# The router inside the attention loop: bias added in PSUM, one batch's operations over more steps, gathers three steps later

## The chip, the cores and the metric

One Trainium2 chip, one of its cores. The metric is the device time of one execution in microseconds (us); the median of several runs counts.

## The reference

Three stages follow each other: masked attention, a mixture of eight experts with a router (top 1), and a dense two-layer block. Cut to what matters here:

```python
# attention: q, k, v are (2, 8, 768, 64); a key counts where its 6-bit bucket equals the query's
mask = q_bucket[:, :, :, None] == k_bucket[:, :, None, :]
scores = np.where(mask, scale * np.matmul(q, k.transpose(0, 1, 3, 2)), -1000000000.0)
attn = np.exp(scores - scores.max(-1, keepdims=True))
attn = attn / (attn.sum(-1, keepdims=True) + 1e-09)
x = (attn @ v).transpose(0, 2, 1, 3).reshape(1536, 512)
# router and experts: x is (1536, 512), w_gate (512, 8), w1 (8, 512, 1024), w2 (8, 1024, 512)
logits = x @ w_gate + modality_bias[modality_id]
e_idx = np.argmax(logits, axis=1)
probs = np.exp(logits - logits.max(-1, keepdims=True))
probs /= probs.sum(-1, keepdims=True) + 1e-09
gate_w = probs[np.arange(N), e_idx]
for e in range(8):
    out[e_idx == e] = gate_w[e_idx == e, None] * (np.maximum(x[e_idx == e] @ w1[e], 0) @ w2[e])
# dense block: w_in (512, 2048), w_out (2048, 512)
h = out @ w_in
y = (np.maximum(h, 0.0) + alpha * np.minimum(h, 0.0)) @ w_out
```

## The kernel before

The attention runs as one loop of 102 steps, `s` from 0 to 101, that is written out by hand. A step takes one block of 128 keys of one head (6 blocks a head, 16 heads, so 96 blocks). For each block TensorE makes two halves of 384 scores (`ST`, tile `st`), ScalarE takes their exponential (`E`, L856) and rounds it to 16 bits (`Eh`, L860), and GpSimd makes the remainder E - Eh (`El`, L861, in `EL`). `EL(s-1)` is issued in step s. From block `ELD` = 88 on the remainder is made by VectorE instead of GpSimd; both of its inputs lie in SBUF. Every second step TensorE multiplies two blocks, Eh and El, with the values (`AV`, tile `av`, L869 to L871), four steps behind. `MAX` (tile `mxp`, L822) makes scores ahead for the row maxima, which VectorE reduces (L823). At the end of a head, `NORM` (L881 to L883) divides.

All small matmuls and transposes of the loop take their PSUM tile from `misc()`, a pool of PM = 2 buffers that also serves the router's scratch: whoever asks for a tile waits until the last user of the tile two requests ago is done. A score tile comes from a pool of five.

At the end of each step runs `hook(s)`. It builds the router (class `Router`) beside the attention. Batch 0 is complete halfway through the loop, so its routing (`first`) is done inside it: a generator that is advanced by one piece at each step listed in `PLAN["first"]`. Its pieces before: `S` (bias, maximum, exponential, argmax) at step 57; nothing at 58; the counting matmuls of `R` at 59; the ranks, counts and `star` (the fullest expert) at 60; `star2` at 63; `adjust` (14 operations on 128x6 elements) at 71; the one-hot matrix `HC` (`onehot`, L273) at 72; `GATE` at 75; `pre` in three pieces at 80, 81 and 83, the last of which writes the token numbers `idp`. GpSimd then gathers the first three tiles of tokens, one indirect DMA each (`GA`, L637), at steps 84, 85 and 87 (`PLAN["ga"]`). `TX0` transposes the gathered tiles at steps 96 and 97 (tile `g`, L602). Steps 91 to 100 also split the first expert's weights on ScalarE and VectorE (`W1`, L610 and L613). `T` and `L` in `hook` transpose x and make the logits `lg` (L182, L185, L196, L200).

Batch 1 is routed after the loop by the same `S`, `R`, `adjust` and `GATE` (tiles `tr`), between the first matmuls of the experts.

Each engine works through its instructions in the order in which they are issued. So a waiting instruction holds everything behind it on its engine. In `S` before, the bias is added by one VectorE operation with both inputs in SBUF, and the result goes to PSUM:

```python
v.tensor_tensor(out=w, in0=self.lg[:, bs], in1=self.tb[:, bs], op=ALU.add)   # L213
```

Of the kernel before, what the change touches and what calls it, by code (L numbers as in the profile page):

```python
# [12 lines left out]
I32 = mybir.dt.int32  # L13
AF = mybir.ActivationFunctionType
ALU = mybir.AluOpType
# [23 lines left out]
PM = 2  # L39
PLAN = dict(  # L40
    v0=(1, 3, 4), T3=(2, 2), Z3=(5, 6), T=(2, 4, 5, 7), Z=(8, 10), ld1=9, ld=0, am1=(12, 12, 13, 13), am=(4, 6, 8,
    10), sc=(13, 15), tot=3, tot0=6, sp=(-2, 4, 10, 18), cap=(3, 2, 0, 1), x=(1, 2, 7, 3), x3=(0, 1, 2, 2), x4=(9, 10, 13, 11), w1=(91, 92, 95, 96, 97, 98, 99, 100), ga=(84, 85, 87), vl=1, am0=(0, 0), Z2=(0, 1), x6=(0, 1, 6, 4), first=(57, 58, 59, 60, 63, 71, 72, 75, 80, 81, 83),
)
NPRE = 3
NT = 22
NBASE = 13
GROUPS = ((0, 1, 2), (3, 4, 5), (6, 7, 8, 9), (10, 11, 12))
NG = NT - NPRE
ELD = 88
LOW = 2.0 ** -15  # L50
HIGH = float(np.uint32(0x47EFFFFF).view(np.float32))

# [5 lines left out]
class Router:  # L58
# [145 lines left out]
    def S(self, b, ps):  # L204
        nc = self.nc
        v = nc.vector
        bs = slice(6 * b, 6 * b + 6)
        s8 = [128, 6, 8]
        p = ps()
        w = p[:, 0:48].rearrange("p (c e) -> p c e", c=6)  # L210
        eq = p[:, 64:112].rearrange("p (c e) -> p c e", c=6)
        pe = p[:, 112:118]
        v.tensor_tensor(out=w, in0=self.lg[:, bs], in1=self.tb[:, bs], op=ALU.add)  # L213
        mx = self.tmp([128, 6, 1], F32, "lmx")
        v.tensor_reduce(out=mx, in_=w, axis=AX.X, op=ALU.max)
        v.tensor_tensor(out=eq, in0=w, in1=mx.to_broadcast(s8), op=ALU.is_equal)
        v.tensor_tensor(out=w, in0=w, in1=mx.to_broadcast(s8), op=ALU.subtract)
        ex = self.tmp(s8, F32, "ex")
        nc.scalar.activation(ex, w, AF.Exp)
        v.scalar_tensor_tensor(out=eq, in0=eq, scalar=-16.0, in1=self.iota16.unsqueeze(1).to_broadcast(s8), op0=ALU.mult, op1=ALU.add)  # L220
        v.tensor_reduce(out=pe, in_=eq, axis=AX.X, op=ALU.min)
        v.tensor_tensor(out=self.oh[:, bs], in0=self.iota[:, 0:8].unsqueeze(1).to_broadcast(s8), in1=pe.unsqueeze(2).to_broadcast(s8), op=ALU.is_equal)
        v.tensor_copy(self.e[:, bs], pe)
        self.ex = ex
        yield
# [101 lines left out]
    def adjust(self, b, ps):  # L327

        v = self.nc.vector
        bs = slice(6 * b, 6 * b + 6)  # L330
        p = ps()
        e, r, pf, rp, f = (p[:, 8 * i:8 * i + 6] for i in range(5))
        si, qi = (p[:, 8 * i:8 * i + 6].bitcast(I32) for i in (5, 6))
        v.tensor_copy(e, self.e[:, bs])
        v.tensor_copy(r, self.r[:, bs])
        isS = self.isS[:, bs]
        v.tensor_scalar(out=isS, in0=e, scalar1=self.es, scalar2=None, op0=ALU.is_equal)
        if b == 0:
            v.scalar_tensor_tensor(out=pf, in0=r, scalar=128.0 * NPRE, in1=isS, op0=ALU.is_lt, op1=ALU.mult)
            v.tensor_scalar(out=self.np_[:, bs], in0=pf, scalar1=-1.0, scalar2=1.0, op0=ALU.mult, op1=ALU.add)  # L340
            v.tensor_tensor(out=isS, in0=pf, in1=isS, op=ALU.not_equal)
        v.tensor_copy(f, isS)
        rps = self.rp[:, bs]
        v.scalar_tensor_tensor(out=rps, in0=f, scalar=self.nm0, in1=self.r[:, bs], op0=ALU.mult, op1=ALU.add)
        v.tensor_copy(si, rps)
        v.tensor_scalar(out=qi, in0=si, scalar1=7, scalar2=None, op0=ALU.logical_shift_right)
        v.tensor_scalar(out=si, in0=si, scalar1=127, scalar2=None, op0=ALU.bitwise_and)
        v.tensor_copy(self.rq[:, bs], qi)
        v.tensor_copy(f, si)
        v.tensor_copy(self.rm[:, bs], si)  # L350
        yield
        self.onehot(self.HC[:, bs], f, 6)

    def pre(self, ps):

        nc = self.nc
        v = nc.vector
        p = ps()
        rq, q, rc = p[:, 256:262], p[:, 264:270], p[:, 288:288 + 6 * NPRE].rearrange("p (c t) -> p c t", c=6)
        v.tensor_copy(rq, self.rq[:, 0:6])  # L360
        s = [128, 6, NPRE]
        v.scalar_tensor_tensor(out=q, in0=self.np_[:, 0:6], scalar=100.0, in1=rq, op0=ALU.mult, op1=ALU.add)
        v.tensor_tensor(out=rc, in0=self.iota[:, 0:NPRE].unsqueeze(1).to_broadcast(s), in1=q.unsqueeze(2).to_broadcast(s), op=ALU.is_equal)
        rv = self.tmp([128, 6, 4, NPRE], F16, "prv")
        s4 = [128, 6, 4, NPRE]
        v.tensor_tensor(out=rv, in0=rc.unsqueeze(2).to_broadcast(s4), in1=self.vals[:, 0:6].unsqueeze(3).to_broadcast(s4), op=ALU.mult)
        yield
        for c in range(6):
            nc.tensor.matmul(p[:, 0:4 * NPRE], self.HC[:, c], rv[:, c].rearrange("p a t -> p (a t)"), start=(c == 0), stop=(c == 5))
        yield  # L370
        self.gates_of(p, NPRE, self.idp, self.gp)
# [125 lines left out]
def _program(base, tc, nc, q, k, v, proj, mod, w_gate, mbias, w1, w2, win, wout, alpha, out):  # L497
# [359 lines left out]
    def EL(s):  # L857
        j=s%6; e,eh,el=E[s]
        if s in (91,94): nc.vector.tensor_copy(eh,e)
        else: nc.scalar.activation(eh,e,AF.Copy)  # L860
        (nc.vector if s>=ELD else nc.gpsimd).tensor_tensor(out=el,in0=e,in1=eh,op=ALU.subtract)  # L861
    av={};xs={}
# [698 lines left out]
```

## Time and profile before

| what | value |
|---|---|
| runs | 692.78, 699.09, 698.83 us; median 698.83 us |
| the profiled execution | 698.25 us, of which the span of its instructions is 696.5 us |
| TensorE busy | 662.4 us, 95% of the span |
| VectorE, ScalarE, GpSimd busy | 450.4 us (65%), 315.8 us (45%), 237.6 us (34%) |
| mean granted clock of TensorE | 0.979 of full speed |

The busy shares are over the whole span. The attention loop takes about the first 262 us; behind it come the experts and then the dense block. A granted clock of 1.00 in a row is 2.4 GHz, 0.50 is 1.2 GHz.

### The profile page before, as it was taken

The numbers are of one execution on the slowest core, as the hardware profiler recorded it, in microseconds if no ns is written. First come the engines' busy times: TensorE is split into PE (matmuls) and PEld (weight loads), VectorE is DVE, ScalarE is ACT, GpSimd is POOL, SyncE is SP. The second block draws the span as 40 slices with busy tenths as digits, with TensorE's granted clock in tenths as the row PEclk, the third lists the DMA queues.
The fourth block names the chain that finished last, engine by engine and source line by source line (L and its number), as shares of the span: only waits on it lengthen the run. The fifth ranks groups of instructions, "written<-read, shape, count | busy, mean of one in ns | idle before, by whom it ended". The sixth has DMA issues, their size and how long they took to land.

```text
span 696.5 us, 12779 instructions
## 1 busy us (share of the span) xinstructions
PE 662.4 (95%) x4938; PEld 562.7 (81%) x4938; DVE 450.4 (65%) x925; ACT 315.8 (45%) x536; POOL 237.6 (34%) x212
## 2 busy tenths in 40 slices
PE   7797999998999899999999999999999999999996
PEld 6586998997878789789888887888888888888884
DVE  6877788788888587846642757999543444443332
ACT  5565797885867863223512337675411111111111
POOL 8775999986966800401000201040030000100002
PEclk9979999999999989999999999999999999999999
DMA  8367855866511309757311643533010000000001
GB/s 215 87 148 173 183 134 115 177 175 145 115 37 49 121 3 333 252 202 276 106 60 61 213 157 130 177 89 128 0 68 24 6 26 0 31 30 1 1 0 60
DMA packets 32859, 75.02 MB, mean 108 GB/s; under 512 B 7276, under 2 KB 7366, under 8 KB 32534
## 3 DMA queue, kind: packets, MB, share of 16 engines
q1 hardware_dynamic: 29700, 64.43, 32.3%
q0 software_dynamic: 2960, 9.70, 4.2%
q8 instruction: 39, 0.64, 0.4%
q14 instruction: 30, 0.25, 0.1%
q10 hardware_dynamic: 130, 0.00, 0.0%
HBM read 49.79 MB, written 14.68 MB: 93 GB/s over the span
## 4 chain that ended last, share of the span: by engine, by line
PE 53%; DVE 1%; ACT 1%; issue 1%; POOL 1%; ACTq 0%; POOLq 0%
PE o L1406 18%; PE h L1380 18%; PE y L1067 8%; PE g L1047 8%; PE tr L1250 1%; POOL out_dram L1423 1%; PE tr L1034 0%; DVE w L1225 0%; DVE op L1225 0%; ACT op L1223 0%; DVE gl L613 0%; ACT gf L1384 0%; ACT q L1385 0%; ACT w L1223 0%; DVE big L1190 0%
## 5 line engine op out<-in xcount | busy, mean ns | idle before, releaser
L861 POOL TENSOR_TENSOR El<-E,Eh 128x768 f16<-128x768 f32 x88 | 144.4, 1651 | 44.1 <-ACT Eh L860 23.2
L856 ACT ACTIVATE E<-st 128x384 f32<-128x384 f32 x192 | 89.2, 492 | 63.1 <-PE st L855 60.8
L823 DVE TENSOR_REDUCE mx<-mxp 128x1 f32<-128x384 f32 x192 | 97.8, 548 | 10.0 <-PE mxp L822 9.2
L610 ACT ACTIVATE gh<-gf 128x512 fp32r<-128x512 f32 x48 | 30.3, 631 | 142.8 <-PE o L1406 132.2
L860 ACT ACTIVATE Eh<-E 128x768 f16<-128x768 f32 x94 | 79.6, 846 | 0.0
L854 PE MATMUL st<-op 97*128 97x384 f32 x192 | 74.8, 390 | 0.6 <-ACT E L856 0.6
L822 PE MATMUL mxp<-op 76*128 76x384 f32 x192 | 66.7, 361 | 7.5 <-DMA op<-big 2.7
L613 DVE TENSOR_TENSOR gl<-gf,gh 128x512 fp32r<-128x512 f32 x48 | 33.1, 690 | 59.2 <-ACT gh L610 59.2
L1423 POOL DMA_INDIRECT out_dram<-x,did x12 | 11.8, 986 | 167.8 <-DVE x L1420 89.1
L1380 PE MATMUL h<-big,op 128*128 128x512 f32 x256 | 67.9, 393 | 0.0
L855 PE MATMUL st<-op 128*128 128x384 f32 x192 | 67.4, 351 | 0.0
L1406 PE MATMUL o<-op,gh 128*128 128x512 f32 x192 | 64.2, 395 | 0.0
L871 PE MATMUL av<-vh,El 128*128 128x65 f16 x576 | 60.0, 197 | 1.9 <-POOL El L861 1.9
L869 PE MATMUL av<-vh,Eh 128*128 128x65 f16 x576 | 60.8, 199 | 0.2 <-DVE big L883 0.2
L870 PE MATMUL av<-vl,Eh 128*128 128x64 f16 x576 | 60.2, 196 | 0.0
L869 PEld LDWEIGHTS <-Eh 128*128 128x128 f16 x576 | 53.7, 100 | 7.7 <-issue 6.4
L1238 POOL DMA_INDIRECT yg<-ys,dpos x10 | 12.2, 1215 | 138.4 <-DVE x L1190 73.0
L1067 PE MATMUL y<-op,hh 128*128 128x512 f32 x172 | 58.7, 399 | 0.0
L1380 PEld LDWEIGHTS h<-big,op 128*128 128x128 f32 x256 | 48.1, 188 | 10.9
L871 PEld LDWEIGHTS <-El 128*128 128x128 f16 x576 | 54.3, 100 | 2.2 <-POOL El L861 2.2
L870 PEld LDWEIGHTS <-Eh 128*128 128x128 f16 x576 | 54.4, 101 | 0.0
L1388 DVE TENSOR_SCALAR gf<-h,al 128x512 f32<-128x512 f32 x33 | 24.8, 751 | 41.7 <-PE h L1380 41.7
(423 smaller groups left out, 1490.7 us busy)
## 6 DMA issues: line engine op xcount, KB each, us to landing
r<-in_moe_w_dram SPq DMA_DIRECT2D x14, 1024.0 KB
op<-B SPq DMA_DIRECT2D x32, 192.0 KB
op<-A SPq DMA_DIRECT2D x28, 192.0 KB
op<-A SPq DMA_DIRECT2D x13, 384.0 KB
ys<-zero SPq DMA_DIRECT2D x19, 256.0 KB
op<-in_moe_w_in_dram SPq DMA_DIRECT2D x4, 1024.0 KB
op<-in_moe_w_out_dram SPq DMA_DIRECT2D x4, 1024.0 KB
ys<-ysb SPq DMA_DIRECT2D x13, 256.0 KB
```

What stands on the lines that cost most here:

```text
L823: nc.vector.tensor_reduce(out=mx[h][:,c,a:a+1],in_=p[:,0:384],axis=AX.X,op=ALU.max)
L854: mm(p[:,0:384],t[0:97,1,js],t[0:97,2,qs],start=True,stop=False)
L855: mm(p[:,0:384],t[:,0,js],t[:,3,qs],start=False,stop=True)
L856: nc.scalar.activation(E[s][0][:,qs],p[:,0:384],AF.Exp,scale=0.125)
L860: else: nc.scalar.activation(eh,e,AF.Copy)
L861: (nc.vector if s>=ELD else nc.gpsimd).tensor_tensor(out=el,in0=e,in1=eh,op=ALU.subtract)
L869: mm(a[:,c*65:c*65+65],eh[:,cs],VH[h//4%2][:,j,h%4,:],start=(j==0 and c==0),stop=False,skip_group_check=True)
L870: mm(a[:,c*65:c*65+64],eh[:,cs],VL[h//4%2][:,j,h%4,:],start=False,stop=False,skip_group_check=True)
L871: mm(a[:,c*65:c*65+65],el[:,cs],VH[h//4%2][:,j,h%4,:],start=False,stop=False,skip_group_check=True)
L1067: nc.tensor.matmul(yps[key][i], a[:, ts], w[:, c], start=(c == 0 and m == 0), stop=(c == 7 and m == 2))
L1380: nc.tensor.matmul(p, terms[t][0][:, kk, cs], terms[t][1][:, kk], start=(n == 0), stop=(n == 11))
L1406: nc.tensor.matmul(po[b][i], a[:, ts], w[:, c % 2], start=(c == 0 and n == 0), stop=(c == 15 and n == 2))
```

## The change

- `S`: `lg` is first copied to the PSUM tile `w`, then `tb` is added there. Holds for both batches.
- `adjust`: in batch 0 a new pause splits it in two, with a new PSUM tile behind it; the one-hot matrix gets a PSUM tile of its own, to which `rm` is copied back. In batch 1 the copy of `r` is no longer made. `pre` takes a new tile for its matmuls.
- `PLAN["first"]`: S at 57, nothing at 58, R at 59 and 60 as before; `star2` at 66 (63 before); `adjust` at 72 and 75 (71); one-hot at 78 (72); `GATE` at 83 (75); `pre` at 84, 85 and 86 (80, 81, 83).
- `PLAN["ga"]`: the gathers at steps 87, 88 and 90 (84, 85, 87).
- `ELD` = 87: the remainder of block 87 too is made by VectorE.

```diff
-    ... ga=(84, 85, 87), ... first=(57, 58, 59, 60, 63, 71, 72, 75, 80, 81, 83),
+    ... ga=(87, 88, 90), ... first=(57, 58, 59, 60, 66, 72, 75, 78, 83, 84, 85, 86),
...
-ELD = 88
+ELD = 87
...
-        v.tensor_tensor(out=w, in0=self.lg[:, bs], in1=self.tb[:, bs], op=ALU.add)
+        v.tensor_copy(w, self.lg[:, bs])
+        v.tensor_tensor(out=w, in0=w, in1=self.tb[:, bs], op=ALU.add)
...
-        e, r, pf, rp, f = (p[:, 8 * i:8 * i + 6] for i in range(5))
-        si, qi = (p[:, 8 * i:8 * i + 6].bitcast(I32) for i in (5, 6))
+        e, r, pf = (p[:, 8 * i:8 * i + 6] for i in range(3))
         v.tensor_copy(e, self.e[:, bs])
-        v.tensor_copy(r, self.r[:, bs])
...
         if b == 0:
+            v.tensor_copy(r, self.r[:, bs])
...
             v.tensor_tensor(out=isS, in0=pf, in1=isS, op=ALU.not_equal)
+            yield
+            p = ps()
+        f = p[:, 24:30]
+        si, qi = (p[:, 8 * i:8 * i + 6].bitcast(I32) for i in (5, 6))
         v.tensor_copy(f, isS)
...
-        v.tensor_copy(f, si)
         v.tensor_copy(self.rm[:, bs], si)
         yield
+        p = ps()
+        f = p[:, 0:6]
+        v.tensor_copy(f, self.rm[:, bs])
         self.onehot(self.HC[:, bs], f, 6)
...
         yield
+        p = ps()
         for c in range(6):
             nc.tensor.matmul(p[:, 0:4 * NPRE], self.HC[:, c], rv[:, c].rearrange("p a t -> p (a t)"), start=(c == 0), stop=(c == 5))
```

## Rows read from the trace of the kernel before

**Rows 1.** The page, part 2: the granted clock in 40 slices of 17.4 us.

```profile
PEclk9979999999999989999999999999999999999999
```

**Rows 2.** Waits of TensorE, 150 to 265 us: waiting line, releaser, us, times, longest.

```profile
PE misc L795 <- DVE r L881: 2.6, 1, 2.6
PE av L871 <- POOL El L861: 1.9, 1, 1.9
...
PE misc L182 <- DVE big L273: 0.8, 1, 0.8
...
PE misc L182 <- DVE big L185: 0.3, 1, 0.3
```

**Rows 3.** Timeline of VectorE around L213: start us, duration us, instruction.

```profile
162.32 2.52 DVE L213 TENSOR_TENSOR misc<-lg,tb 128x48 f32<-128x48 f32 x1
164.88 0.21 DVE L215 TENSOR_REDUCE lmx<-misc 128x6 f32<-128x48 f32 x1
...
166.48 0.16 DVE L223 COPY e<-misc 128x6 f32<-128x6 f32 x1
...
266.56 0.22 DVE L213 TENSOR_TENSOR tr<-lg,tb 128x48 f32<-128x48 f32 x1
```

**Rows 4.** Timeline of GpSimd, three stretches; in brackets the idle time before.

```profile
158.28 6.49 POOL L861 TENSOR_TENSOR El<-E,Eh 128x768 f16<-128x768 f32 x4
...
196.48 3.36 POOL L861 TENSOR_TENSOR El<-E,Eh 128x768 f16<-128x768 f32 x2 [1.74 <-PE mxp L822]
...
235.26 0.98 POOL L637 DMA_INDIRECT big<-x_d,idp  x1 [0.17 <-issue]
236.26 3.26 POOL L861 TENSOR_TENSOR El<-E,Eh 128x768 f16<-128x768 f32 x2
239.68 1.51 POOL L637 DMA_INDIRECT big<-x_d,idp  x1 [0.16 <-issue]
241.20 1.65 POOL L861 TENSOR_TENSOR El<-E,Eh 128x768 f16<-128x768 f32 x1
```

**Rows 5.** Timeline of VectorE, 196 to 206 us.

```profile
198.71 0.15 DVE L334 COPY misc<-e 128x6 f32<-128x6 f32 x1
...
199.36 0.17 DVE L339 SCALAR_TENSOR_TENSOR misc<-misc,isS 128x6 f32<-128x6 f32 x1
...
202.40 0.94 DVE L273 TENSOR_TENSOR big<-iota,misc 128x768 f16<-128x768 f32 x1
```

**Rows 6.** Stretches: length, busy us of each engine, granted clock, DMA share, GB/s.

```profile
164.20:166.80 2.60, 0.01 (x1) 0.04 (x2) 2.13 (x9) 1.18 (x4) 0.56 (x1) 1.00 1.00 214
168.20:171.60 3.40, 3.40 (x45) 3.10 (x45) 3.31 (x7) 1.71 (x3) 2.27 (x2) 0.50 0.00 0
...
200.00:206.00 6.00, 4.50 (x65) 3.56 (x64) 5.63 (x19) 3.40 (x7) 3.25 (x2) 1.00 0.11 18
...
243.30:250.10 6.80, 6.80 (x67) 6.31 (x64) 5.95 (x10) 3.48 (x7) 0.00 (x0) 0.50 0.02 5
```

**Rows 7.** Timeline of VectorE: where it waited after 170 us and after 238 us.

```profile
172.64 1.09 DVE L823 TENSOR_REDUCE mx<-mxp 128x1 f32<-128x384 f32 x2 [1.09 <-PE mxp L822]
...
238.74 1.60 DVE L861 TENSOR_TENSOR El<-E,Eh 128x768 f16<-128x768 f32 x1 [1.56 <-ACT Eh L860]
...
241.65 2.03 DVE L861 TENSOR_TENSOR El<-E,Eh 128x768 f16<-128x768 f32 x1 [0.84 <-ACT Eh L860]
...
249.04 0.96 DVE L861 TENSOR_TENSOR El<-E,Eh 128x768 f16<-128x768 f32 x1 [0.68 <-ACT Eh L860]
...
252.78 0.96 DVE L861 TENSOR_TENSOR El<-E,Eh 128x768 f16<-128x768 f32 x1 [0.62 <-ACT Eh L860]
```

**Rows 8.** Timeline of ScalarE: the rounding of block 87.

```profile
236.25 0.85 ACT L860 ACTIVATE Eh<-E 128x768 f16<-128x768 f32 x1
```

**Rows 9.** Timeline of TensorE: the first transposes of gathered tokens.

```profile
253.71 1.07 PE L602 MATMUL g<-ident,big 128*128 128x128 f32 x8
```

**Rows 10.** Instructions on tile idp: time from the gathers' issue to landing.

```profile
DMA to landing us min/median/max: 3.3/3.6/4.0
```

More of the change, by code (lines that the diff above doesn't have):

```diff
@@ L41 @@
     v0=(1, 3, 4), T3=(2, 2), Z3=(5, 6), T=(2, 4, 5, 7), Z=(8, 10), ld1=9, ld=0, am1=(12, 12, 13, 13), am=(4, 6, 8,
-    10), sc=(13, 15), tot=3, tot0=6, sp=(-2, 4, 10, 18), cap=(3, 2, 0, 1), x=(1, 2, 7, 3), x3=(0, 1, 2, 2), x4=(9, 10, 13, 11), w1=(91, 92, 95, 96, 97, 98, 99, 100), ga=(84, 85, 87), vl=1, am0=(0, 0), Z2=(0, 1), x6=(0, 1, 6, 4), first=(57, 58, 59, 60, 63, 71, 72, 75, 80, 81, 83),
+    10), sc=(13, 15), tot=3, tot0=6, sp=(-2, 4, 10, 18), cap=(3, 2, 0, 1), x=(1, 2, 7, 3), x3=(0, 1, 2, 2), x4=(9, 10, 13, 11), w1=(91, 92, 95, 96, 97, 98, 99, 100), ga=(87, 88, 90), vl=1, am0=(0, 0), Z2=(0, 1), x6=(0, 1, 6, 4), first=(57, 58, 59, 60, 66, 72, 75, 78, 83, 84, 85, 86),
 )
```

## The prediction

> **What bounds the kernel now.** I read the busy shares first: TensorE is busy nearly throughout, so a change on the other engines can move the time only where TensorE waits for them, or where its clock falls. The row of the granted clock [rows 1] is next: in the attention (the first 15 slices) it dips in few places, the last of them in the slice from 244 us. Then come TensorE's waits over the stretch in which the router runs beside the attention [rows 2]. Two stand out, and both end at engines that the change touches: 2.6 us for VectorE at a `misc` tile, and 1.9 us for GpSimd's remainder El. The others are below 1.2 us; two of them, 0.8 and 0.3 us, are again for `misc` tiles that VectorE has not given back.
>
> The first wait is explained by one instruction. L213, the addition of the bias, took 2.52 us in the loop and 0.22 us after it [rows 3], for the same shape. In the loop GpSimd was making four remainders without a pause, from 158.28 to 164.77 us [rows 4], and L213 ended at 164.84, right behind them. So an operation of VectorE with both inputs in SBUF waits here until GpSimd's stream ends. A later case agrees: VectorE's remainder that starts at 241.65 took 2.03 us instead of the 0.96 of its fellows [rows 7], and GpSimd's last remainder ended at 242.85 [rows 4], 0.83 us before it. Operations with one input in PSUM do not wait: the copy L334 (0.15 us) and L339 (0.17 us) ran at 198.71 and 199.36 [rows 5], inside a GpSimd pair of remainders that lasted from 196.48 to 199.84 [rows 4].
>
> What L213 holds up is S, whose last reader L223 ends at 166.64 [rows 3]; TensorE's Z matmul needs S's `misc` tile and stands from 164.18 to 166.79 [rows 2, 6]. Soon after, the granted clock is 0.50 (1.2 GHz) from 168.2 to 171.6 us, with TensorE busy all of it [rows 6]. The second wait has the same sequel: GpSimd does gather, remainders 85 and 86, gather, remainder 87 in its order [rows 4]; remainder 87 ends at 242.85, TensorE stands for 1.9 us [rows 2], and from 243.3 to 250.1 us the clock is 0.50, TensorE again busy throughout [rows 6]. Each sequel is work at half rate: 3.4 us that could be 1.7, and 6.8 us that could be 3.4.
>
> **The change part by part.** The sum is made against the profiled execution, 698.25 us; that is 0.6 us below the median of the three runs.
>
> *Bias in PSUM.* L213 becomes a copy (SBUF to PSUM) and an addition with one PSUM input. Both are forms that rows 5 show unhindered beside GpSimd. From L213 to L215 went by 2.56 us [rows 3]; two instructions at 0.25 each, the spacing of such small ones (0.22 us run [rows 3], plus a few hundredths), make 0.5. S then ends 2.05 us earlier, and TensorE's 2.61 us wait shrinks to 0.55. Term A: -2.05 us. Bounds: nothing if the copy waits for GpSimd as the addition did, 2.61 if S were done in time altogether.
>
> *Half clock after it.* With 0.55 us of wait I expect no fall: the 1.5 us that TensorE is idle from 200 to 206 us left the clock at 1.00 [rows 6]. On TensorE alone that gives 1.7 us. But VectorE is busy 3.31 of those 3.4 us [rows 6], and its next idle time is the 1.09 us before 172.64 [rows 7], behind which it is loaded again; it can come forward by A and this idle time, no more. Term B: -1.09 us, bounds 0 and -1.70.
>
> *Operations spread.* adjust is 14 operations in one go, from 198.71, the first of rows 5, until 201.5; after two row maxima the one-hot of 0.94 us follows [rows 5], and TensorE waits 0.8 us for the tile that this chain holds and then 0.3 for the next [rows 2]. After the change six operations come at step 72, seven at 75, and the one-hot at 78 with a tile of its own; no tile is held over several steps. The work itself is the same 14 operations and the one-hot, some 3.9 us at these durations; star2, GATE and pre also only move to later steps, GATE and pre behind the last row maxima, where VectorE has room: before remainder 88 alone it stood 1.56 us [rows 7]. Term C: -1.0 us, the two waits. Bounds: 0 (each new tile brings a wait of its own, since there are still two) and -1.5, all that TensorE is idle in that stretch [rows 6].
>
> *Gathers later and remainder 87 on VectorE.* GpSimd's last remainder is now 86, and no gather stands ahead of any. Eh of block 87 is there at 237.10 [rows 8]. VectorE is free then (idle until 238.74 [rows 7]); GpSimd, without its gathers of about 1 to 1.5 us each [rows 4], has finished remainders 85 and 86 by about 237.3. So El 87 takes 0.96 us [rows 7] and is there by about 238.3, hidden in the 1.56 us of idle time; if a GpSimd remainder is still running, add up to 1.65 [rows 4], which the next idle time of 0.84 covers only in part. TensorE asked for it at 241.0. The wait of 1.88 us goes, and with it, I expect, the half clock: 1.88 + 3.40 = 5.28 us on TensorE. It can't have all of that, since VectorE is next: from 241.65 to the loop's end it is nearly always busy. What it can shed is the wait inside the remainder that starts at 241.65 (2.03 - 0.96 = 1.07) and its three idle times behind it, 0.68, 0.64 and 0.62, of which rows 7 show the first and the last: 3.0 us together. Term D: -3.0 us, bounds -1.07 and -5.28.
>
> What is queued behind the moved instructions: behind the gathers on GpSimd nothing of the loop any more; behind El 87 on VectorE remainder 88 and a transposed copy. The gathers land 3.6 us after issue [rows 10]; issued three steps later, at about 238 to 242, the last lands by about 246, and TX0 begins at 253.71 [rows 9], or some 7 us earlier once everything has moved. That still holds. In batch 1, behind the loop, S gets one copy and adjust loses one, at about 0.2 each: nothing.
>
> Sum: 698.25 - 2.05 - 1.09 - 1.0 - 3.0 = 691.1 us. After the loop nothing is tied to absolute time, since its loads are issued there; so I let the whole sum arrive at the end.
>
> A rule that speaks against the later gathers: the Trainium skill, page "SBUF — State Buffer", section "SBUF: two separate sides", says that GpSimd can't write the descriptors of its DMAs while VectorE runs an operation that takes their shared ports. The gathers now meet VectorE's remainders, so by this rule they come later. The trace has one such meeting: the gather at 239.68, beside a remainder of VectorE until 240.34, took 1.51 us against 0.98 for the one at 235.26 [rows 4, 7], 0.5 us more. Three such meetings are 1.6 us, which the distance to TX0 covers. What a stronger form would do is the last rival.
>
> **The rivals.** *Only the waits, not the clock, and the gain is taken back by VectorE and ScalarE.* The steps between 172 and 241 us are close to balanced, and an earlier TensorE may just wait more often there. Then A and the smaller end of D remain, 2.05 + 1.07, and some 0.5 of B and C: about 694.6 us. For it: VectorE's 5.63 busy of 6 us from 200 to 206 [rows 6]. Against it: VectorE waited for TensorE at 172.64 [rows 7] and GpSimd for it at 196.48 [rows 4], so they have slack too.
>
> *More than the sum.* If VectorE's order lets TensorE have all of B and C and most of D, the upper bounds give 2.05 + 1.70 + 1.5 + about 4.5 = 9.75, or 688.5 us. The run at 692.78 among the three of before speaks for it: something of the order of 6 us comes and goes with nothing changed, about the 5.1 us of both half-clock stretches, and the waits would then still be there to be removed.
>
> *The change doesn't do what it says.* The copy reads SBUF in single precision; if it waits for GpSimd like L213, A and B vanish and a copy is added: 698.25 - 1.0 - 3.0 + 0.2 = 694.5 us. The copy L334 [rows 5] speaks against it.
>
> *Slower: the gathers starve.* From 244.66 until about 261 us VectorE runs two-input operations on SBUF nearly back to back (remainders, weight splits). If a gather can't get in between them at all, the three come after 261 us and land at about 261 + 3 x 1.0 + 3.6 = 268 instead of before 253.71 [rows 4, 9, 10]; TX0, and behind it everything on TensorE, waits 14 us. With the 7.2 gained elsewhere that is 705 us. It begins to cost when the last gather lands later than TX0, some 2 to 8 us later than I reckon, and ends slower than before from about twice 7 us. Against it stand the 1.51 us of the gather that met a remainder [rows 4].
>
> **How the numbers follow.** About 1% of 698.8 us, 7 us, is what a measurement can tell from no change. Chances: the forecast (689.5 to 693) 0.50, the gain taken back 0.24, more than the sum 0.16, the copy that waits 0.05, the starving gathers 0.05. Predicted time 691.1 us. Range 687.5 to 695.5: from the upper bounds to the taken-back gain and the copy that waits. The forecast lies just at 1% faster than the median, so its half and the larger gain make faster 0.48, the rest and the two cases near 694.5 make the same 0.47, slower 0.05.
>
> **What the profile afterwards would show.** L213's copy and addition at about 0.2 us each with GpSimd busy beside them; no wait of 2 us at L795; granted clock 1.00 in the slices behind 160 and behind 240 us; remainder 87 on VectorE at about 1 us, no TensorE wait for GpSimd's El; gathers unbroken behind GpSimd's last remainder; the loop's end (the last NORM) at about 255 instead of 261 us. The prediction is wrong if the copy takes over 1 us, if a new TensorE wait of 2 us or more stands between 200 and 240 us and brings the clock down again, or if L602 waits for a gather.

## The result and the profile after

The changed kernel takes 689.29 us (median; 687.33 to 690.03), the kernel before 698.46 us in the same comparison: ratio 0.9887, 95% interval 0.9853 to 0.9922, so 0.8 to 1.5% faster. A second comparison gave 689.46 us and 0.9892 (0.9850 to 0.9935). The profiled execution took 690.03 us, its span is 688.2 us; the prediction was 691.1 us.

The waits of TensorE in the same stretch of the changed kernel (lines are 1 to 7 higher, since the file has grown):

```profile
PE mxp L829 <- ACT E L863: 1.4, 3, 0.5
PE av L876 <- DVE big L890: 1.3, 1, 1.3
PE g L590 <- DVE op L613: 0.8, 1, 0.8
PE tr L182 <- DVE big L890: 0.7, 1, 0.7
...
PE misc L802 <- DVE r L888: 0.6, 1, 0.6
```

The two waits on which the prediction rested [rows 2] are 0.6 us (it was 2.6) and gone. The longest single one left is new: the product `av` of head 15 waits for VectorE's division of head 14. The waits for the one-hot's tile (0.8 and 0.3) are gone as well. The first line, three short waits for ScalarE, was there before too, with 1.5 us in all.

VectorE at the bias, the answer to [rows 3]:

```profile
162.40 0.19 DVE L213 COPY misc<-lg 128x48 f32<-128x48 f32 x1
162.69 0.22 DVE L214 TENSOR_TENSOR misc<-misc,tb 128x48 f32<-128x48 f32 x1
162.94 0.21 DVE L216 TENSOR_REDUCE lmx<-misc 128x6 f32<-128x48 f32 x1
...
164.55 0.16 DVE L224 COPY e<-misc 128x6 f32<-128x6 f32 x1
```

GpSimd, the answer to [rows 4]:

```profile
158.35 6.49 POOL L868 TENSOR_TENSOR El<-E,Eh 128x768 f16<-128x768 f32 x4
...
229.44 3.26 POOL L868 TENSOR_TENSOR El<-E,Eh 128x768 f16<-128x768 f32 x2 [1.37 <-ACT Eh L867]
232.88 1.69 POOL L644 DMA_INDIRECT big<-x_d,idp  x1 [0.18 <-issue]
234.87 0.97 POOL L644 DMA_INDIRECT big<-x_d,idp  x1 [0.30 <-issue]
236.14 0.95 POOL L644 DMA_INDIRECT big<-x_d,idp  x1 [0.30 <-issue]
```

GpSimd's four remainders run as before, at the same time and with the same 6.49 us; the copy and the addition run beside them at 0.19 and 0.22 us, where one addition took 2.52. The gathers stand behind the last remainder, in one go.

And the granted clock over the whole execution, the answer to [rows 1]:

```profile
PEclk9979999999999999999999999999999999999998
```

The dip in the slice from 244 us is gone in this execution.

Where the time came from is read best from three events on VectorE: the start of the bias in S, the division of head 13 and that of head 15, the last of the loop. Before, L213 starts at 162.32 [rows 3], and the divisions at

```profile
234.88 0.23 DVE L881 TENSOR_SCALAR r<-av,sc 128x6 f32<-128x6 f32 x1 [1.64 <-PE av L875]
...
260.88 0.22 DVE L881 TENSOR_SCALAR r<-av,sc 128x6 f32<-128x6 f32 x1
```

(timeline of VectorE, kernel before), after the change at

```profile
230.20 0.23 DVE L888 TENSOR_SCALAR r<-av,sc 128x6 f32<-128x6 f32 x1 [0.89 <-PE av L882]
...
252.65 0.22 DVE L888 TENSOR_SCALAR r<-av,sc 128x6 f32<-128x6 f32 x1
```

So S to head 13 took 72.56 us and takes 67.80 (4.76 less), head 13 to head 15 took 26.00 and takes 22.45 (3.55 less). What follows until the end of the span is 435.6 and 435.55 us: nothing is lost or won behind the loop. The sum of the two, 8.3 us, is the difference of the spans.

### The profile page after: what moved, and what is told of

It reads as the page before. It is cut to its first block, busy times and chain, and to the rows that moved or that the text cites. A ratio compares the mean times of both kernels' runs of the same rounds, so it can differ in the third digit from the quotient of the medians.

```text
span 688.2 us, 12777 instructions
## 1 busy us (share of the span) xinstructions
PE 658.1 (96%) x4938; PEld 558.1 (81%) x4938; DVE 446.9 (65%) x927; ACT 315.2 (46%) x536; POOL 235.8 (34%) x211
## 4 chain that ended last, share of the span: by engine, by line
PE 54%; DVE 1%; ACT 1%; issue 1%; POOL 1%; ACTq 0%; POOLq 0%
PE o L1413 19%; PE h L1387 18%; PE y L1074 8%; PE g L1054 8%; PE tr L1257 1%; POOL out_dram L1430 1%; PE tr L1041 0%; DVE w L1232 0%; DVE op L1232 0%; ACT op L1230 0%; DVE gl L620 0%; ACT gf L1391 0%; ACT q L1392 0%; ACT w L1230 0%; DVE big L1197 0%
## 5 line engine op out<-in xcount | busy, mean ns | idle before, releaser
L868 POOL TENSOR_TENSOR El<-E,Eh 128x768 f16<-128x768 f32 x87 | 142.8, 1655 | 38.9 <-ACT Eh L867 20.5
L620 DVE TENSOR_TENSOR gl<-gf,gh 128x512 fp32r<-128x512 f32 x48 | 33.1, 690 | 59.2 <-ACT gh L617 57.2
L876 PE MATMUL av<-vh,Eh 128*128 128x65 f16 x576 | 58.9, 197 | 1.3 <-DVE big L890 1.3
L876 PEld LDWEIGHTS <-Eh 128*128 128x128 f16 x576 | 52.8, 99 | 8.5 <-issue 6.1
L877 PE MATMUL av<-vl,Eh 128*128 128x64 f16 x576 | 58.4, 194 | 0.0
L878 PE MATMUL av<-vh,El 128*128 128x65 f16 x576 | 58.2, 195 | 0.0
L877 PEld LDWEIGHTS <-Eh 128*128 128x128 f16 x576 | 53.4, 99 | 0.0
```

The source lines that it names most:

```text
L876: mm(a[:,c*65:c*65+65],eh[:,cs],VH[h//4%2][:,j,h%4,:],start=(j==0 and c==0),stop=False,skip_group_check=True)
L877: mm(a[:,c*65:c*65+64],eh[:,cs],VL[h//4%2][:,j,h%4,:],start=False,stop=False,skip_group_check=True)
L878: mm(a[:,c*65:c*65+65],el[:,cs],VH[h//4%2][:,j,h%4,:],start=False,stop=False,skip_group_check=True)
```

## The experiments

Single executions of one kernel differ: the 72 of the kernel before that ran beside the experiments lie between 692.96 and 702.09 us. Each has a mean granted clock with it, and the two go together (correlation -0.93): 693.04 at 0.990, 702.09 at 0.974. One straight line with a common slope through 169 executions of all kernels (one of 2297 us, at a clock of 0.283, is left out) gives 0.35 us of time for each us that the clock was at half rate; what it leaves over scatters by 0.95 us. So each kernel has two figures below: its median, and its difference from the kernel before at an equal mean clock, with the 95% half-width of the fit; between two of the other kernels the half-width is 0.8 to 1.1 us. The stage lengths are from one profile each, with the time at half clock in them, which comes as 0, 3.4 or 6.8 us.

| kernel | median us | at equal clock, us | S to head 13 (half clock) | head 13 to 15 (half clock) |
|---|---|---|---|---|
| before | 696.78 (72 executions) | 0 | 72.56 (3.4) | 26.00 (6.8) |
| changed | 689.30 (10) | -6.3 ± 0.6 | 67.80 (0), again 67.75 (0) | 22.45 (0), again 22.83 (3.4) |
| x1 bias in PSUM alone | 694.42 (10) | -1.7 ± 0.6 | 69.66 (0) | 26.00 (6.8) |
| x2 late gathers alone | 695.48 (10) | -1.2 ± 0.6 | 71.31 (0) | 22.72 (0) |
| x3 remainder 87 on VectorE alone | 697.36 (10) | -1.2 ± 0.6 | 71.30 (0) | 24.73 (6.8) |
| x4 spread and late gathers | 693.42 (10) | -3.3 ± 0.6 | 71.55 (6.8) | 22.72 (0) |
| x5 changed, bias from SBUF | 690.89 (4) | -3.5 ± 1.0 | 71.67 (6.8) | 24.03 (6.8) |
| x6 changed, remainder 87 on GpSimd | 690.35 (8) | -5.6 ± 0.7 | 67.81 (0) | 22.69 (0) |
| x7 before, own tile for S | 697.46 (10) | -0.4 ± 0.6 | 73.20 (6.8) | 23.81 (0) |

**x1: the bias in PSUM alone.**

```diff
-        v.tensor_tensor(out=w, in0=self.lg[:, bs], in1=self.tb[:, bs], op=ALU.add)
+        v.tensor_copy(w, self.lg[:, bs])
+        v.tensor_tensor(out=w, in0=w, in1=self.tb[:, bs], op=ALU.add)
```

> Only the bias: the kernel before with the copy into PSUM and the addition there. My theory (the addition with two SBUF inputs waits for GpSimd's stream, and the wait costs TensorE time and then half clock): the copy and the addition take about 0.2 us each, the 2.6 us wait at L795 falls to about 0.6, the clock stays at 1.00 behind it, and what follows comes 2.7 us earlier, also at the loop's end: about 695.7 us beside 698.5. The 1.9 us wait for GpSimd's El of block 87 and the half clock behind it stay. Rival (the steps from 172 to 241 us are balanced and take the gain back): within 0.7 us of before at the loop's end.

Measured: ratio 0.9963 (0.9936 to 0.9989). Waits of TensorE:

```profile
PE av L872 <- POOL El L862: 1.9, 1, 1.9
...
PE misc L796 <- DVE r L882: 0.6, 1, 0.6
```

The wait fell as expected, the one for GpSimd's El stayed, and the stage up to head 13 is 2.9 us shorter than in the kernel before, and 1.65 us shorter than in x2 and x3, which have the old addition and no half clock. So the wait itself is worth 1.65 us, and the 3.4 us of half clock in the profile of before another 1.25.

**x2 and x3: the two edits at block 87, one at a time.**

```diff
-... ga=(84, 85, 87)
+... ga=(87, 88, 90)      # x2
-ELD = 88
+ELD = 87                 # x3
```

> Only the gathers at steps 87, 88, 90; remainder 87 stays on GpSimd. My theory (the gathers in front of GpSimd's last remainders make El 87 late): only one gather now stands ahead of El 87, which ends at about 240.3 instead of 242.85, before TensorE asks for it at 241.0; wait and half clock go, the loop ends about 3 us earlier, 695.5 us. Rival (it is the move of El 87 to VectorE that matters): the 1.9 us wait stays or moves, no change, 698.5 us.

> Only remainder 87 on VectorE, gathers at their old steps. My theory: VectorE starts El 87 at about 237.2 but must wait for GpSimd's pair 85 and 86, which the second gather holds back to 239.5, so El 87 is there at about 240.5, just before TensorE asks at 241.0; the wait goes or is under 0.5 us, the half clock goes too, about 2.5 us gained, 696 us. Rival (both parts are needed): VectorE falls behind by the 3.3 us of that operation, TensorE waits for a VectorE remainder instead, with half clock behind it: 698 to 700 us.

Measured: 0.9994 (0.9961 to 1.0027) and 1.0003 (0.9970 to 1.0037), no difference in the ratios; 1.2 us each at equal clock. GpSimd in x2:

```profile
234.77 3.27 POOL L861 TENSOR_TENSOR El<-E,Eh 128x768 f16<-128x768 f32 x2 [0.44 <-ACT Eh L860]
238.22 1.18 POOL L637 DMA_INDIRECT big<-x_d,idp  x1 [0.18 <-ACT E L856]
239.44 1.67 POOL L861 TENSOR_TENSOR El<-E,Eh 128x768 f16<-128x768 f32 x1
```

El 87 is the single remainder. It ends 5.6 us after the division of head 13 (235.55 in x2), against 8.0 in the kernel before, and TensorE no longer waits for it. In x3 VectorE did wait for GpSimd's pair, and longer than a single remainder lasts; VectorE first, then GpSimd:

```profile
233.81 3.15 DVE L861 TENSOR_TENSOR El<-E,Eh 128x768 f16<-128x768 f32 x1 [1.27 <-ACT Eh L860]
236.89 0.54 DVE L185 COPY big<-misc 128x384 f32<-128x384 f32 x1
```

```profile
232.88 3.26 POOL L861 TENSOR_TENSOR El<-E,Eh 128x768 f16<-128x768 f32 x2
```

VectorE's El 87 began in the first of the pair and came out 0.8 us after the second (236.14). In x3 a new wait of 1.3 us for VectorE (at L196) took the old one's place, with 6.8 us of half clock behind it. In x2 TensorE waits for VectorE too, at L869 (the division of head 14) and at L196, with no half clock behind it in this profile:

```profile
PE av L869 <- DVE big L883: 1.5, 2, 1.3
...
PE misc L196 <- DVE lg L200: 0.7, 1, 0.7
```

The kernel before waits at L869 for at most 0.2 us and at L196 not at all; x7, which has the wait for El 87 without half clock, waits 1.0 us at L869. Both edits are worth the same where the other is missing, since each by itself removes the wait for El 87, and shorter ones for VectorE come instead. The size that both expectations gave, 2.5 to 3 us, was too large: it contained the half clock, and it did not reckon with these waits.

**x4: the spread, with the late gathers, which it needs.** The changed kernel with the bias added from SBUF and `ELD = 88`.

> The operations spread over more steps, with the late gathers (which it needs), but the bias still added from SBUF and remainder 87 on GpSimd. My theory (spreading by itself takes away the TensorE waits at the one-hot's tile and leaves VectorE less loaded before 230 us): about 2 us more than the late gathers alone, 693.5 us. Rival (the 2 us between 196 and 235 us came from the earlier S, spreading gives nothing alone): the same as the late gathers alone.

Measured: 0.9952 (0.9923 to 0.9981); at equal clock 2.1 ± 0.8 us more than x2. The stage up to head 13 is no shorter than in x2, but it has 6.8 us of half clock, x2 none. Spreading is worth about 2 us by itself; the rival falls.

**x5 and x6: one part of the change taken back.** x5 has the old addition in the changed kernel, x6 has `ELD = 88`.

> The changed kernel with the bias added from SBUF again. My theory: the addition takes about 2.5 us beside GpSimd's remainders, TensorE waits 2.6 us for the tile; 1.7 us more than the changed kernel at an equal mean clock, plus what half clock comes behind the wait by chance (up to 2 us): about 691.5 us beside 689.3. Rival (with the operations spread, VectorE has room and the wait is made good before 230 us): the same as the changed kernel, within 0.5 us at equal clock.

> The changed kernel with remainder 87 back on GpSimd. My theory, as the late gathers alone now show it: one gather ahead of El 87 still lets it end before TensorE asks; the stretch from the NORM of head 13 to that of head 15 is 0.3 us longer than in the changed kernel (22.7 against 22.4 us), the time the same within 0.5 us at equal clock. Rival (the move of El 87 is worth something on its own): 1 us or more slower.

Measured: 690.89 and 690.35 us. At equal clock x5 gives back 2.8 ± 1.1 us of the 6.3: the wait is 2.6 us again, and VectorE's greater room does not make it good. x6 gives back 0.75 ± 0.9 us at equal clock, which is not clear of zero; its stage from head 13 to 15 is 22.69 against 22.45, just as forecast. With the gathers late, moving remainder 87 is worth a few tenths, by that stage.

**x7: what does the blocked addition hold up?** The kernel before, where only S takes its tile from the five score tiles:

```diff
-            R["first"] = rr.first(misc)
+            R["first"] = rr.first(misc, GP)
...
-    def first(self, ps):
-        yield from self.S(0, ps)
+    def first(self, ps, ps0):
+        yield from self.S(0, ps0)
```

> The kernel before, but S takes its PSUM tile from the pool of five score tiles instead of the two misc tiles; the bias is still added from SBUF and VectorE still waits for GpSimd. Theory (TensorE's wait is for the tile that S holds): the 2.6 us wait at L795 goes, and as VectorE catches up later, about half of the gain of the copy comes, 0.8 us at equal clock. Rival (what costs is VectorE's queue, since row maxima, z rows and score tiles stand behind the blocked addition): TensorE waits 2 us or more at a score tile or at the same matmul for a later VectorE operation, no gain.

Measured: 1.0017 (0.9984 to 1.0051), no gain, as the rival said. The wait at L795 is gone, but TensorE waits elsewhere at the same place; first its timeline, then VectorE's, then ScalarE's:

```profile
164.94 0.45 PE L854 MATMUL st<-op 97*128 97x384 f32 x1 [1.02 <-ACT E L856]
...
166.93 0.69 PE L822 MATMUL mxp<-op 76*128 76x384 f32 x1 [0.49 <-ACT E L856]
```

```profile
161.00 2.52 DVE L213 TENSOR_TENSOR g<-lg,tb 128x48 f32<-128x48 f32 x1
```

```profile
164.29 0.21 ACT L219 ACTIVATE ex<-g 128x48 f32<-128x48 f32 x1 [3.00 <-DVE g L217]
164.40 0.48 ACT L856 ACTIVATE E<-st 128x384 f32<-128x384 f32 x1
```

S's exponential stands in ScalarE's queue behind the blocked addition, waits 3.00 us, and the exponentials of the scores stand behind it; so the score tiles come back late. The tile was only where TensorE met the delay first. What costs is the blocked instruction at the head of VectorE's queue, and through `ex` of ScalarE's. One thing is left open: S now holds one of the five score tiles itself, which may have added to these waits, and no run separates the two.

**x9 to x11 and two repeats: a version that is faster still?** In the changed kernel VectorE sets the loop's end, and GpSimd is idle. x9 gives three of the eight weight remainders to GpSimd; x10 also moves all eight later, by one to three steps; x11 moves them and leaves them on VectorE.

```diff
-            W1(i // 4, i % 4, i % 4 + 1)
+            W1(i // 4, i % 4, i % 4 + 1, nc.gpsimd if i in (4, 5, 6) else nc.vector)   # x9, x10
-    ... w1=(91, 92, 95, 96, 97, 98, 99, 100)
+    ... w1=(94, 95, 96, 97, 98, 99, 100, 101)                                          # x10, x11
```

> The changed kernel with three of the eight weight remainders (steps 97 to 99) on GpSimd, which is idle from 237 us. In the changed kernel VectorE sets the end of the loop (busy 14.7 of the 15 us before 254). Theory: these three of 0.63 us leave VectorE just ahead of the last NORM, which comes up to 1.9 us earlier; TensorE's wait of 0.7 us for it goes: 0.7 to 1.3 us faster at equal clock, 688.3 us. Rival (two-input operations of VectorE and GpSimd exclude each other, so that VectorE waits for GpSimd's longer ones, or GpSimd's pieces come too late for the experts' first matmuls): no gain, or up to 1 us slower.

> The changed kernel with the eight weight pieces at steps 94 to 101 instead of 91 to 100, and the remainders of the fifth to seventh (steps 98 to 100) on GpSimd. In the changed kernel two pieces (1.3 us of VectorE) stand ahead of the NORM of head 14, for which TensorE waits 1.27 us, the longest wait left in the loop, with half clock behind it in some executions. Theory: that wait goes to under 0.3 us, and the two waits at the loop's end (0.8 and 0.7) stay away as with the three pieces on GpSimd: 1.5 to 2.5 us faster than the changed kernel at equal clock, about 687 us. Rival (the work only moves: VectorE is late for the pieces that the experts' first matmuls need, and TensorE waits there): within 0.5 us of the changed kernel, or slower.

> The changed kernel with the weight pieces at steps 94 to 101, all on VectorE. Theory: the 1.27 us wait for the NORM of head 14 goes, but the same 1.3 us of VectorE's work comes back before the last NORM, where VectorE sets the end of the loop: the waits there grow to 1.5 us or more, and the time is within 0.7 us of the changed kernel at equal clock. Rival: VectorE's freed time is enough, and it is as fast as with three pieces on GpSimd.

> The changed kernel itself beside the kernel before and the next one on one chip, for a closer figure and a second profile. My theory (waits that are gone in every execution, half clock that comes by chance): 6 us faster than before at equal mean clock, and again no half clock between S and the last NORM or less than in most profiles of the kernel before; S to the last NORM 90.3 us if there is none. Rival (the 9 us were partly luck of few executions): under 5 us in the medians.

> Three weight remainders on GpSimd again, beside the changed kernel. Its profile had lost the two last waits of the loop (1.5 us together) but had 3.4 us of half clock behind another wait. Theory: without that, S to the last NORM is 87.5 us, and at equal clock it is 1.0 to 1.5 us faster than the changed kernel. Rival: the waits come back behind the loop; no difference.

Measured: x9 688.49 us, and again (y2) 690.31 beside 689.46 for the changed kernel (y1); x10 690.15; x11 688.14 (ratios to before 0.9875, 0.9889, 0.9920, 0.9892). At equal clock, against the kernel before: -6.2 for x9 with y2, -4.7 for x10, -5.9 for x11, against -6.3 for the changed kernel. At equal clock none is faster than it, and x9 and x11 do not differ from it clearly. In x9 and y2 the last division of the loop came 1.5 and 2 us nearer to S (88.8 and 88.3 us, changed 90.25), but the rest of the span grew by nearly as much (437.1 and 437.3 against 435.55): in x9 VectorE's next operation then waited 1.8 us for ScalarE, and TensorE 0.5 us for it. x10 shows why sharing with GpSimd costs; VectorE, then GpSimd:

```profile
248.29 1.28 DVE L613 TENSOR_TENSOR op<-g,op 128x512 fp32r<-128x512 f32 x2
249.49 1.76 DVE L620 TENSOR_TENSOR op<-r,op 128x512 fp32r<-128x512 f32 x1
251.18 0.68 DVE L613 TENSOR_TENSOR op<-g,op 128x512 fp32r<-128x512 f32 x1
```

```profile
249.44 2.94 POOL L620 TENSOR_TENSOR op<-r,op 128x512 fp32r<-128x512 f32 x2 [11.90 <-ACT op L617]
```

The same operation, 0.69 us elsewhere, took 1.76 beside GpSimd's, and TensorE waited 2.2 us for the L613 that stood behind it. The expectations of x9, x10 and y2 had it wrong, their rivals right. y1 bears its theory out: 6.8 us between the medians and, with the first four executions, 6.3 at equal clock; its second profile has 3.4 us of half clock. In x11 the wait for the division of head 14 fell from 1.3 to 0.7 us, and the one at L590 rose from 0.8 to 1.1: the work moved.

## Why the prediction was right, point by point

- *The addition waits for GpSimd, the copy does not.* Shown: 2.52 us became 0.19 and 0.22 beside the same GpSimd stream; x5 brings 2.6 us of wait back. Term A was -2.05; the wait alone is worth 1.65 us by stage lengths, 1.7 by x1 at equal clock. The saving on VectorE is as large as forecast (2.02 us from L213 to the maximum: 2.56 became 0.54), but not all of it arrives. That S's tile is what passes the delay on was wrong as an explanation (x7): it passes by the queues as well. (Of the two operations that the prediction took as precedents, L334 reads SBUF and writes PSUM, as the new copy does; only L339 has an input in PSUM.)
- *Half clock behind the waits.* The prediction took it as a certain sequel; it is a matter of chance. The same 2.6 us wait was followed by 3.4 us of it in the profile of before, by none in x2 and x3, by 6.8 us in x4 and x5. Term B (-1.09) was about what the 3.4 us cost (1.25), for that one execution.
- *The spread.* Term C, -1.0, was too small, by these figures even its bound of -1.5: 1.9 us between x1 and the changed kernel in the stage up to head 13 (69.66 to 67.80, both without half clock), 2.1 us between x2 and x4 at equal clock. The prediction counted only the two waits that it saw; taking star2, GATE and the pieces of adjust out of the stretches where VectorE was loaded may have given the rest. This last attribution was argued from the profile and not separated by a run.
- *Block 87.* Term D, -3.0, was the right size for the profile (3.55) by adding two things: about 1.1 us for the wait, which x7 (23.81, wait present, no half clock) and x2 (22.72) show (1.1 and not 1.9, since x2 waits 0.7 us longer at L196 and 0.3 at L869 than x7), with 0.25 more for remainder 87, and 2.2 us for 6.8 us of half clock (26.00 in before against 23.81). At equal clock it is the smallest of the three parts. Remainder 87 ran on VectorE in 0.99 us beside the end of GpSimd's pair, as reckoned.
- *Behind the loop nothing changes.* Shown by every kernel but those that move the weight pieces: 435.4 to 435.7 us from the last division to the end.
- *The rivals.* The gain was not taken back: the largest part of it sits in the balanced steps up to head 13. The copy did not wait. The gathers did not starve: one of three was held, 1.69 us beside a VectorE remainder against 0.97 and 0.95 for the others, and no transpose waited for them. The trap that the Trainium skill describes (page "SBUF — State Buffer", section "SBUF: two separate sides") is of VectorE operations in a two-port mode, and the section says that `tensor_tensor`, which a remainder is, has none; so the prediction read that rule too widely. All the same, the first gather, which began 0.6 us before the end of a remainder, took 0.7 us longer than the others, and the third, in which one began (at 236.69), did not; what the first waited for is not shown.

The time came out near the forecast by the forecast's mechanism, but that it came so near is in part luck: A was 0.4 us too large and C about 1 us too small, and B and a part of D count half clock, of which the profile of before happened to have 10.2 us between S and the last division.

The sum of the parts alone at equal clock is 1.7 + 2.1 + 1.2 and some tenths, 5 to 5.8 us, beside 6.3 for the whole; the difference is within the half-widths. Most of the rest of the 7.5 us between the medians is less time at half clock: its mean in the changed kernel is 22.5 us in an execution, in the kernel before 25.4, 2.9 us that cost 1.0 at 0.35. The stage from S to head 13 fits this: of the six profiles with the blocked addition four have half clock there, of the eight with the bias in PSUM none.

## What to carry to other kernels

Look for one operation that takes many times what the same line takes elsewhere: here a 0.22 us addition with both inputs in SBUF stood 2.5 us behind a GpSimd stream, and a copy into PSUM first, one instruction more, freed it. A transfer that is issued from a compute engine's queue belongs behind the last operation there that anyone waits for. When a kernel's executions differ by more than the effect, note the clock with each time and compare at equal clock, or compare stage lengths between two events, since a wait's sequel at half clock comes and goes by itself.

## What the runs showed of the hardware that was not expected

- VectorE does not always get in between two GpSimd operations that follow each other. In x3 it waited over the boundary of a pair of remainders until both were done (3.15 us for an operation of 0.96); L213 did so before [rows 3, 4]. The Trainium skill (page "SBUF — State Buffer", section "SBUF: two separate sides") calls the shared ports an exclusive lock that one instruction holds to its end; these two cases were longer than one instruction. In x10 it did get in: its L620 ended at 251.25, while the second of GpSimd's pair ran until 252.39 and took 1.72 us, the first 1.26. So "until GpSimd's stream ends", as the prediction reads L213, holds for the cases that it read and not for every one; what decides is not shown.

```profile
250.67 1.72 POOL L620 TENSOR_TENSOR op<-r,op 128x512 fp32r<-128x512 f32 x1
```

- The fall of the clock is not tied to a wait of a given length. A wait of 2.6 us was followed by no fall in x2, and by one in x5; TensorE's rows behind it, for each (length, busy us of the engines, granted clock near the end):

```profile
166.10:168.70 2.60, 0.00 (x0) 0.02 (x1) 2.15 (x9) 1.16 (x4) 0.59 (x1) 1.00 1.03 217
168.70:176.00 7.30, 7.29 (x116) 6.44 (x116) 7.06 (x22) 5.81 (x11) 4.55 (x3) 1.00 0.14 28
```

```profile
165.50:166.88 1.38, 0.00 (x1) 0.03 (x1) 1.02 (x6) 1.17 (x4) 0.00 (x0) 0.62 0.95 206
165.90:172.70 6.80, 5.82 (x49) 4.93 (x50) 5.51 (x15) 3.73 (x8) 2.36 (x2) 0.50 0.20 43
```

  In x5 TensorE went back to work at 166.88; the clock had already fallen by then (0.62 on the mean from 165.50). And behind a wait of only 1.28 us the clock fell for 3.4 us in the second profile of the changed kernel:

```profile
244.10:247.40 3.30, 2.96 (x41) 2.96 (x42) 3.27 (x7) 0.87 (x2) 0.00 (x0) 0.54 0.00 0
```

- Half clock costs less than half of its time here: 0.35 us for each us over all executions, where 0.5 would be the most. Between profiles of one stage it differs, from 0.37 (1.25 us for 3.4, before against x2 up to head 13) and 0.32 (2.2 for 6.8, before against x7 behind it) down to 0.11 (0.38 for 3.4, y1 against the changed kernel). A part of it shows in the waits: x7, which has the wait for El 87 but no half clock behind it, has a further one for VectorE, at L869, where the kernel before, with 6.8 us of half clock, has none over 0.2 us.

```profile
250.04 0.20 PE L869 MATMUL av<-vh,Eh 128*128 128x65 f16 x1 [1.00 <-DVE big L883]
```

  It fits that VectorE and ScalarE catch up while TensorE runs at 1.2 GHz; no run was made to show it.
